# Fused attention and gated MLP: w_out reaches the DRAM scratch whole and early, and the maxima get other places in VectorE's order

## The chip, the cores and the metric

One core of a Trainium2 chip runs the kernel. The metric is the device time of one execution in microseconds. The kernel before was timed three times: median 730.39 us, from 729.67 to 731.17.

## What is computed

For 8 batches of 8 heads, 576 tokens and head width 64, a pack of 32 queries `p` attends to the tokens, and the tokens then attend to that pack. The result, laid out as 4608 x 512, goes through a gated MLP with d_ff = 2048.

```python
p_packed = sm_attn(p, k, v)
out = sm_attn(q, p_packed, p_packed)
x = out.transpose(0, 2, 1, 3).reshape(B * S, H * D)
h = x @ w_in
sp = np.maximum(h, 0.0) + np.log1p(np.exp(-np.abs(h)))     # softplus
return (h * erf(sp)) @ w_out
```

## The kernel before

**Units.** The second attention is folded into the first weight: W' = packed values times `w_in` (`wp`, L545), and h = a2 W' (L592). A unit is a batch b, a half c of its tokens and a block i of 256 columns of d_ff; `step(n, ...)` computes h of unit n, starts its gate and adds the products of earlier gates with `w_out` into the output accumulators (`o_part`, L644). An operand is split into a high and a low part, and a product is three matmuls.

**Two regimes.** Batches 0 and 1 (units 0 to 31) take softplus and erf from the tables in groups (L607, L610, gate L614) and fp32r splits of `w_out`: `wohl[f]` holds `wo_hi[f]` and `wo_lo[f]`, f = 0 to 15. Batches 2 to 7 take a gate of three tanh (L673 to L682) and 16-bit splits `woh[i]`, two blocks f to each. The 16-bit splits need scales: the largest absolute value of `w_in` (`tops_in`), of `w_out` (`tops_out`) and of the batch's packed values (`norm`). A maximum is gathered on DVE (`gather`), turned to a row by a PE transpose and cut to a power of two (`turn`), and spread over the partitions by a matmul (`spread`). `rho` scales W' of a batch, `sigma` the whole of `w_out`.

**How w_out comes and goes.** A block is loaded into a staging tile, its buffer `wo[f]` is cleared on POOL (L154), ACT casts the upper words (L123), DVE sets the rest (L127), and `split_w_out_high` and `split_w_out_low` make the parts. `wo`, `wohl`, the staging tiles, and later `wox` and `woh`, share the 18 buffers tagged "wo". In steps 20 to 23 `save` writes the block to a DRAM scratch: the high part by a DMA on SP, the low part by an accumulating DMA on POOL over the same rows. `whole` (L244) reads two blocks back as `wox[i]` in steps 24 to 27, and `halve` (L249 on ACT, L250 on DVE) makes `woh[i]`.

**Order.** `BEGINNING` is an order written out by hand for the work of units 0 to 19. After it, `plan` hangs parts on four slots of a step: slots 0 and 1 behind the first accumulation of the step, slot 3 behind the third, slot 2 at the step's end; `ATTEND` does it for the attention of a batch. PE, DVE and ACT keep the order in which the program issues their work; SP keeps it in BEGINNING only. POOL's order is a scheduler's. The outputs of batches 0 and 1 leave by DMAs on POOL (`outT<-ob`, L659 and L661), those of the second turn accumulating; `ob` has four buffers. The PSUM pool `ps_h` has two banks for h, for rows and columns of the maxima, and for some of the attention's scores; `ps_m` holds one tile.

Of the kernel before, what the change touches and what calls it, by code (L numbers as in the profile page):

```python
# [8 lines left out]
F32 = mybir.dt.float32  # L9
# [6 lines left out]
ALU = mybir.AluOpType  # L16
# [25 lines left out]
K12 S12 W1.3 W1.2 o11.0 o10.1 o11.1 o10.3 h15.0 H1.3 L14 F15 s14 V1.3 H1.2 T12 h15.1 L13 o11.3 p11.1 m12 U12 d15.1 M0 C  # L42
o10.2 o11.2 v12 c15.0 s15 h16.0 p11.2 p11.0 h16.1 c16.1 K14 m13 R14 o12.2 d16.0 s16 K13 S13 u13 v13 p11.3 e14 T13
o12.1 h17.0 h19.0 d19.0 o12.0 m14 e15 V1.2 m15 o12.3 e16 U14 v14 L15 K15 h17.1 c17.1 o13.1 o13.0 h19.1 c17.0 C c19.1
S15 o13.3 o14.1 h18.0 h18.1 m16 s19 s17 d18.0 C C C d18.1 M1 M2 M3 s18 e18 U15 o14.0 m18 e19 v15 e17 o13.2 o14.2 T15 m19 o14.3
m17 T14
"""

# [2 lines left out]
def tile_pack_attention_moe(ctx: ExitStack, tc: tile.TileContext, qT, kT, v, pT, w_in, w_out, outT):  # L51
    nc = tc.nc
    P = 128
    B, _, NC, S = qT.shape
    DFF = w_in.shape[1]
# [15 lines left out]
    NB0 = 2  # L71
# [9 lines left out]
    apool = ctx.enter_context(tc.tile_pool(name="attn", bufs=2))  # L81
# [10 lines left out]
    ones = cpool.tile([1, P], F32, name="ones")  # L92
    w_in_sb = cpool.tile([P, 4, DFF], F32, name="w_in_sb")
    scratch = dpool.tile([DFF, DM], F32, name="scratch")
    wo, wo_hi, wo_lo = {}, {}, {}
# [63 lines left out]
    def split_w_out_high(f, copy=nc.vector.tensor_copy):  # L159
        both = opool.tile([P, 2, DM], F32R, name=f"wohl{f}", tag="wo")  # L160
        wo_hi[f], wo_lo[f] = both[:, 0, :], both[:, 1, :]
        copy(wo_hi[f], wo[f])

    def split_w_out_low(f):
        nc.vector.tensor_tensor(wo_lo[f], wo[f], wo_hi[f], op=ALU.subtract)

    tops, inverse, halved, pairs = {}, {}, {}, {}
    rho, omega, gate_scales = {}, {}, {}

    def tallest(kind, k, src):  # L170

        if kind not in tops:
            tops[kind] = cpool.tile([P, 8 if kind == "in" else 16], F32, name=f"tops_{kind}")
        nc.vector.tensor_reduce(tops[kind][:, k:k + 1], src, axis=AX.X, op=ALU.max, apply_absolute_value=True)

    def tallest_in(k):

        tallest("in", k, w_in_sb[:, k // 2, (k % 2) * 2 * FB:(k % 2 + 1) * 2 * FB])

    def two_over(dst, src):  # L180

        nc.vector.tensor_reduce(dst, src, axis=AX.X, op=ALU.max)
        nc.vector.tensor_scalar(dst, dst, TINY, None, op0=ALU.max)
        bits = dst.bitcast(U32)
        nc.vector.tensor_scalar(bits, bits, EXPONENT, EXPONENT, op0=ALU.bitwise_and, op1=ALU.bitwise_xor)
# [22 lines left out]
    def other_way(dst, src):  # L208

        nc.vector.tensor_scalar(dst.bitcast(U32), src.bitcast(U32), EXPONENT, None, op0=ALU.bitwise_xor)  # L210

    def scales(b):

        rho[b] = apool.tile([P, 1], F32, name=f"rho{b}", tag="rho")
        nc.vector.tensor_scalar(rho[b][:], inverse[b][:], inverse["in"][:], 2.0 ** 11, op0=ALU.mult, op1=ALU.mult)
        back = apool.tile([P, 1], F32, name=f"back{b}", tag="back")
        other_way(back[:], rho[b][:])
        gate_scales[b] = apool.tile([P, 2], F32, name=f"gs{b}", tag="gs")
        nc.vector.tensor_scalar(gate_scales[b][:], consts[:], back[:], None, op0=ALU.mult)
        inverse[b] = back  # L220
# [8 lines left out]
    def out_weights():  # L229
# [1 line left out]
        nc.vector.tensor_scalar(sigma[:], inverse["out"][:], 2.0 ** 13, None, op0=ALU.mult)  # L231
        inverse["sigma"] = cpool.tile([P, 1], F32, name="inv_sigma")
        other_way(inverse["sigma"][:], sigma[:])

    def save(f):

        rows = scratch[f * P:(f + 1) * P, :]
        nc.sync.dma_start(rows, wo_hi[f].bitcast(F32))
        nc.gpsimd.dma_start(rows, wo_lo[f].bitcast(F32), accum_op=ALU.add)  # L239

    def whole(i):

# [14 lines left out]
    def in_turn(ins):  # L257

        if functions:
# [8 lines left out]

    ATTEND = {
# [52 lines left out]
    def attention(b):  # L322

        joined, third, roomy = b > NB0, b == NB0, b == 0
# [3 lines left out]
        def chunk(name, tag="kvq"):  # L328
            if tag == "kvq":
                return apool.tile([P, S], F32, name=f"{name}_{b}", tag="kvq", bufs=6)[:]  # L330
            if tag == "wo":
                return opool.tile([P, S], F32, name=f"{name}_{b}", tag="wo")[:]
            return tpool.tile([P, S], F32, name=f"{name}_{b}", tag=tag)[:]

        def bank(name, single=False):

            if single:
                return [ps_h.tile([P, 512], F32, name=f"{name}_{b}_{x}", tag="ps_h")[:] for x in range(2)], None
            if name in at_o:
                d = at_o[name]  # L340
                return [ps_o.tile([P, 512], F32, name=f"{name}_{b}_{x}", tag=f"ps_o{d + x}")[:] for x in range(2)], None
            ps = ps_m.tile([P, 2, 512], F32, name=f"{name}_{b}", tag="ps_m")
            return [ps[:, 0, :], ps[:, 1, :]], ps
# [10 lines left out]
        p = apool.tile([P, NC, NK], F32, name=f"p{b}", tag="p")  # L354
        nc.sync.dma_start(p[:], pT[b])
        k = [chunk(f"k{c}") for c in range(NC)]
# [76 lines left out]
        if roomy:  # L433
# [7 lines left out]
            po, pr = bank("p")[0]  # L441
# [56 lines left out]
        if b >= NB0:  # L498
            one = apool.tile([1, 1], F32, name=f"one{b}", tag="one")
            two_over(one[:], po[0:1, P:2 * P])  # L500
            yield
            nc.tensor.matmul(po[:, 2 * P:2 * P + 1], ones[:], one[:], start=True, stop=True)
            inverse[b] = apool.tile([P, 1], F32, name=f"inv{b}", tag="inv")
            nc.vector.tensor_copy(inverse[b][:], po[:, 2 * P:2 * P + 1])
        yield
        ta = apool.tile([P, 2, S], F32, name=f"ta{b}", tag="big", bufs=3)
        for c2 in range(2):
            banks = bank(f"s2_{c2}", b > NB0 + 1 or (b >= NB0 and c2 == 0) or (b == 1 and c2 == 1))
            for c in range(NC):
                for r in range(2):  # L510
                    nc.tensor.matmul(banks[0][r][NK * c:NK * c + NK, 0:HT], ptt[64 * r:64 * r + 64, NK * c:NK * c + NK],
                                     q[c][64 * r:64 * r + 64, c2 * HT:(c2 + 1) * HT], start=True, stop=True)
            yield
            if roomy:
                scores.append(banks[0])
            else:
                for r in range(2):
                    nc.vector.transpose(ta[:, r, c2 * HT:(c2 + 1) * HT], banks[0][r][:, 0:HT])
                yield
        tb = apool.tile([P, 2, S], F32, name=f"tb{b}", tag="big", bufs=3)  # L520
        kind = F32R if b < NB0 else F16
# [37 lines left out]
    def w_prime_high(b, j, copy=nc.scalar.copy):  # L559
        for hi, lo, ps in w_prime_parts(b, j):  # L560
            if b < NB0:
                copy(hi, ps)
            else:
                nc.scalar.mul(hi, ps, rho[b][:])
# [8 lines left out]
    raw, gs, rows, banks_of, ts = {}, {}, {}, {}, {}  # L573
# [205 lines left out]
    def slot(n, where):  # L779
        return plan.setdefault((n, where), [])  # L780

    for b in range(NB0, B):
        for j in range(NFB):
            n = JOINS[b][j] if b in JOINS else first_use[b] + (JOINS_LATER if b < B - 1 else PAIRED)[j]
# [6 lines left out]
            slot(n, where).append((attend, b))  # L791

    for k in range(4, 2 * NC):
        slot(19 + k // 2, 2).append((tallest_in, k))
    f = 0
    for n, count in ((22, 4), (23, 1), (24, 3), (25, 3), (27, 2), (28, 3)):
        for f in range(f, f + count):
            slot(n, 2).append((lambda f: tallest("out", f, wo_hi[f].bitcast(F32)), f))
        f += 1
    for n, where, part, kind in ((23, 2, gather, "in"), (24, 1, turn, "in"), (25, 0, spread, "in"),  # L800
                                 (28, 2, gather, "out"), (29, 1, turn, "out"), (30, 0, spread, "out")):
        slot(n, where).insert(0 if part == spread else len(slot(n, where)), (part, kind))
    slot(25, 2).insert(0, (scales, NB0))
    slot(30, 0).append((out_weights,))
    slot(32, 3).append((out_scale, NB0))
    for f in range(DFF // P):
        slot(20 + f // 4, 1).append((save, f))
    for i in range(NBLK):
        slot(24 + i // 2, 1).append((whole, i))
        slot(30 + i, 2).append((halve, i))  # L810
    for b in range(NB0 + 1, B):
        slot(first_use[b] - 6, 1).append((scales, b))
        slot(first_use[b] - 6, 1).append((out_scale, b))
# [29 lines left out]
    def fetch(*which):  # L843
# [4 lines left out]
        "N": lambda: next(halves["N"]), "X": lambda: next(halves["X"]),  # L848
        "F": fetch, "L": lambda *w: fetched[w][0](), "K": lambda *w: fetched[w][1](),
        "S": split_w_out_high, "T": split_w_out_low,  # L850
        "W": w_prime, "H": w_prime_high, "V": w_prime_low,
        "h": h_half, "c": h_copy, "s": softplus, "e": erf, "m": gate, "u": split_high, "v": split_low,
        "d": lambda n, k: h_copy(n, k, nc.vector.tensor_copy), "U": lambda n: split_high(n, nc.scalar.copy),
        "R": lambda f: split_w_out_high(f, nc.scalar.copy), "G": lambda b, j: w_prime_high(b, j, nc.vector.tensor_copy),
        "o": o_part, "p": put, "i": keep_busy, "M": tallest_in,
    }
    start = len(traced)
    for word in BEGINNING.split():
# [47 lines left out]
```

## Time and profile before

| What | us |
|---|---|
| median of 3 runs | 730.39 (729.67 to 731.17) |
| the profiled execution | 729.6 |
| its span | 727.8 |
| PE busy | 687.0 (94%) |
| DVE busy | 596.9 (82%) |
| ACT busy | 562.6 (77%) |
| POOL busy | 50.6 (7%) |
| mean granted PE clock | 0.981 |

The span is that of the instructions of the profiled execution; 1.8 us of its time lie around it. Busy shares are means over the whole span; the beginning, the stretch from 150 to 215 us and the regime of the tanh gates differ much from each other.

### The profile page before, as it was taken

To read this page: it belongs to the slowest core of one execution; us is meant where nothing else is said; L and a number is where in the kernel's file an instruction comes from. 1 tells how busy PE (TensorE), PEld (TensorE's weight loads), DVE (VectorE), ACT (ScalarE), POOL (GpSimd) and SP (SyncE) were. 2 spreads that over 40 slices of the span, in tenths; PEclk is the share of its full clock that TensorE was granted. 3 is DMA by queue.
4 is the path that set the end of the run, shared out by engine and by line. 5 is a ranking of instruction groups with operands and counts; after the bars stand their busy time and mean duration, and the time that the engine had idled before them with its cause. 6 is when DMAs were issued, how large, how long until landed. Compare 5 with 4: busy or idle time off the path is not lost.

```text
span 727.8 us, 15690 instructions
## 1 busy us (share of the span) xinstructions
PE 687.0 (94%) x6458; PEld 542.5 (75%) x6458; DVE 596.9 (82%) x945; ACT 562.6 (77%) x987; POOL 50.6 (7%) x75
## 2 busy tenths in 40 slices
PE   8899999988469989999999999999999999999997
PEld 6588989967459867786767777776767777677775
DVE  4999998687347799988997889888997889978775
ACT  2899888946167968988889778888889778878784
POOL 2011111123401100000000000000000000000000
PEclk9999999999779999999999999999999999999999
DMA  9955543299933230222011310222001200001000
GB/s 321 398 203 178 185 141 123 88 316 291 249 53 64 33 129 24 82 83 92 3 39 53 116 62 9 78 82 83 14 33 54 83 2 9 25 1 34 2 33 32
DMA packets 37639, 71.00 MB, mean 98 GB/s; under 512 B 4288, under 2 KB 13504, under 8 KB 37568
## 3 DMA queue, kind: packets, MB, share of 16 engines
q1 hardware_dynamic: 31904, 60.50, 24.6%
q0 software_dynamic: 5376, 8.92, 6.9%
q8 instruction: 50, 0.82, 0.5%
q10 hardware_dynamic: 288, 0.59, 0.2%
q14 instruction: 21, 0.17, 0.1%
HBM read 49.81 MB, written 20.19 MB: 96 GB/s over the span
## 4 chain that ended last, share of the span: by engine, by line
PE 39%; DVE 27%; ACT 21%; issue 6%; DMA 4%; POOL 2%; SPq 0%; POOLq 0%; ACTq 0%; DVEq 0%
PE o L644 22%; PE h L592 12%; DVE t L677 6%; DVE t L678 6%; ACT t L675 4%; ACT t L673 4%; DVE gl L627 3%; ACT u L676 3%; ACT t L680 3%; PE wp L545 3%; DVE hs L682 2%; POOL scratch L239 2%; DVE gh L620 2%; DMA wi<-w_in 2%; ACT ob L656 1%
## 5 line engine op out<-in xcount | busy, mean ns | idle before, releaser
L644 PE MATMUL o<-gh,woh 128*128 128x288 f16 x1536 | 304.9, 287 | 0.9 <-ACT ob L656 0.9
L644 PEld LDWEIGHTS <-woh 128*128 128x128 f16 x2304 | 223.8, 98 | 67.8 <-issue 11.7
L644 PE MATMUL o<-gl,woh 128*128 128x288 f16 x768 | 219.9, 286 | 0.5 <-DVE gl L627 0.4
L592 PE MATMUL h<-a2h,wph 128*128 128x288 f16 (+1 forms) x512 | 149.5, 292 | 3.9 <-ACT hs L600 2.7
L592 PE MATMUL h<-a2h,wpl 128*128 128x288 f16 (+1 forms) x512 | 148.5, 290 | 1.2 <-DVE wpl L569 1.2
L592 PE MATMUL h<-a2l,wph 128*128 128x288 f16 (+1 forms) x512 | 148.2, 289 | 0.0
L677 DVE SCALAR_TENSOR_TENSOR t<-hs,gs,t 128x576 f32<-128x576 f32 x96 | 78.1, 814 | 50.1 <-ACT u L676 49.5
L644 PE MATMUL o<-gh,wohl 128*128 128x288 f32 x448 | 100.2, 304 | 0.0
L602 ACT ACTIVATE hs<-h 128x288 f32<-128x288 f32 x192 | 71.7, 407 | 34.1 <-PE h L592 30.2
L627 DVE TENSOR_TENSOR gl<-hs,gh 128x576 f16<-128x576 f32 (+1 forms) x124 | 93.9, 758 | 4.8 <-ACT gh L620 0.8
L680 ACT ACTIVATE t<-t 128x576 f32<-128x576 f32 x96 | 65.8, 685 | 40.0 <-DVE t L678 38.6
L592 PEld LDWEIGHTS <-wph 128*128 128x128 f16 x768 | 74.7, 98 | 20.6 <-issue 1.6
L644 PEld LDWEIGHTS o<-gh,wohl 128*128 128x128 f32 x448 | 76.0, 192 | 5.8 <-issue 3.1
L678 DVE SCALAR_TENSOR_TENSOR t<-u,t 128x576 f32<-128x576 f32 x96 | 72.8, 758 | 3.3
L673 ACT ACTIVATE t<-hs,gs 128x576 f32<-128x576 f32 x96 | 73.8, 769 | 0.0
L682 DVE SCALAR_TENSOR_TENSOR hs<-t,hs 128x576 f32<-128x576 f32 x96 | 71.9, 749 | 1.0 <-ACT t L680 1.0
L620 DVE CAST gh<-hs 128x576 f16<-128x576 f32 (+1 forms) x117 | 53.3, 455 | 21.1 <-PE o L644 20.8
L675 ACT ACTIVATE t<-t 128x576 f32<-128x576 f32 x96 | 65.6, 683 | 3.0
L676 ACT ACTIVATE u<-t 128x576 f32<-128x576 f32 x96 | 65.6, 683 | 3.1
L644 PE MATMUL o<-gl,wohl 128*128 128x288 f32 x224 | 67.2, 300 | 0.0
L592 PEld LDWEIGHTS <-wpl 128*128 128x128 f16 x384 | 37.7, 98 | 9.7
L644 PEld LDWEIGHTS o<-gl,wohl 128*128 128x128 f32 x224 | 43.2, 193 | 0.3 <-DVE gl L627 0.2
(134 smaller groups left out, 834.7 us busy)
## 6 DMA issues: line engine op xcount, KB each, us to landing
q<-qT SPq DMA_DIRECT2D x32, 288.0 KB, 4.3
k<-kT SPq DMA_DIRECT2D x30, 288.0 KB, 5.0
wos<-w_out SPq DMA_DIRECT2D x16, 512.0 KB, 6.0
outT<-ob SPq DMA_DIRECT2D x48, 144.0 KB, 1.8
v<-v SPq DMA_DIRECT2D x24, 256.0 KB, 4.3
wi<-w_in SPq DMA_DIRECT2D x12, 512.0 KB, 6.4
outT<-ob POOLq DMA_DIRECT2D x32, 144.0 KB, 3.3
scratch<-wohl SPq DMA_DIRECT2D x16, 256.0 KB, 5.9
```

The costliest lines, as they stand in the source:

```text
L592: nc.tensor.matmul(ps[:, 0:HT], w[:, r, fo:fo + P], a[:, r, c * HT:(c + 1) * HT], start=(m == 0), stop=(m == 5))
L602: nc.scalar.mul(dst, src, 2.0 ** -19)
L620: copy(ghi[:], gs[n][0][:])
L627: nc.vector.tensor_tensor(glo[:], hs[:], ghi[:], op=ALU.subtract)
L644: nc.tensor.matmul(acc[b, c, d][:, 0:HT], w[f][:, d * P:(d + 1) * P], gg[:, k, :], start=(first and k == 0 and m == 0), stop=(last and k = ...
L673: nc.scalar.activation(t[:], hs[:], AF.Tanh, bias=T_BIAS, scale=scale[:, 0:1])
L675: nc.scalar.activation(t[:], t[:], AF.Square, bias=root * Q_BIAS, scale=root * Q_SCALE)
L676: nc.scalar.activation(u[:], t[:], AF.Tanh, bias=U_BIAS, scale=U_SCALE / A2)
L677: nc.vector.scalar_tensor_tensor(t[:], hs[:], scale[:, 1:2], t[:], op0=ALU.mult, op1=ALU.add)
L678: nc.vector.scalar_tensor_tensor(t[:], u[:], A1, t[:], op0=ALU.mult, op1=ALU.add)
L680: nc.scalar.activation(t[:], t[:], AF.Tanh, bias=A_BIAS, scale=A_SCALE)
L682: nc.vector.scalar_tensor_tensor(hs[:], t[:], 1.0, hs[:], op0=ALU.add, op1=ALU.mult)
```

## The change

Each block `wo[f]` goes to the scratch whole, by one plain DMA on POOL issued right behind the cast to its high part; the 16 writes on SP and the 16 accumulating DMAs on POOL of steps 20 to 23 are gone. The maxima get earlier places: two of `w_out` stand in BEGINNING, the others mostly a step or a slot earlier, `gather` of both kinds and `scales(2)` too, and `halve` moves to another slot of its step. In batch 2 the matmul that spreads the norm (`spread_norm`) is issued behind the first half of the second attention's scores, not ahead of it.

```diff
-S15 ... h18.1 m16 s19 s17 ...
+S15 ... h18.1 m16 O0 O1 s19 s17 ...
...
         copy(wo_hi[f], wo[f])
+        nc.gpsimd.dma_start(scratch[f * P:(f + 1) * P, :], wo[f])
...
+    def tallest_out(f):
+        tallest("out", f, wo_hi[f].bitcast(F32))
...
+    def spread_norm(b, po, one):
+        nc.tensor.matmul(po[:, 2 * P:2 * P + 1], ones[:], one[:], start=True, stop=True)
+        inverse[b] = apool.tile([P, 1], F32, name=f"inv{b}", tag="inv")
+        nc.vector.tensor_copy(inverse[b][:], po[:, 2 * P:2 * P + 1])
...
-    def save(f):
-        rows = scratch[f * P:(f + 1) * P, :]
-        nc.sync.dma_start(rows, wo_hi[f].bitcast(F32))
-        nc.gpsimd.dma_start(rows, wo_lo[f].bitcast(F32), accum_op=ALU.add)
...
             two_over(one[:], po[0:1, P:2 * P])
-            yield
-            nc.tensor.matmul(po[:, 2 * P:2 * P + 1], ones[:], one[:], start=True, stop=True)
...
+            if not third:
+                yield
+                spread_norm(b, po, one)
...
+            if third and c2 == 0:
+                spread_norm(b, po, one)
...
-        slot(19 + k // 2, 2).append((tallest_in, k))
+        slot(19 + k // 2, 1).append((tallest_in, k))
...
-    for n, where, part, kind in ((23, 2, gather, "in"), (24, 1, turn, "in"), (25, 0, spread, "in"),
-                                 (28, 2, gather, "out"), (29, 1, turn, "out"), (30, 0, spread, "out")):
+    for n, where, part, kind in ((22, 1, gather, "in"), (23, 1, turn, "in"), (24, 1, spread, "in"),
+                                 (28, 1, gather, "out"), (29, 1, turn, "out"), (30, 0, spread, "out")):
...
-    slot(25, 2).insert(0, (scales, NB0))
+    slot(24, 2).append((scales, NB0))
...
-        slot(20 + f // 4, 1).append((save, f))
...
-        slot(30 + i, 2).append((halve, i))
+        slot(30 + i, 3 if i == 0 else 1).append((halve, i))
```

**POOL, from the outputs of batch 0 in BEGINNING on.** Before, the last clearing of a `wo` buffer and eight outputs stand ahead of the saves of the low parts:

```order
L154 MEMSET wo_1385 128x512
L154 MEMSET wo_1405 128x512
L661 DMA outT<-ob_0_3_1_1414 128x288
L661 DMA outT<-ob_0_3_2_1458 128x288
L661 DMA outT<-ob_0_3_0_1461 128x288
L661 DMA outT<-ob_0_3_3_1493 128x288
L154 MEMSET wo_1545 128x512
L661 DMA outT<-ob_1_3_0_1723 128x288
```

With the change the saves stand between them:

```order
L154 MEMSET wo_1398 128x512
L154 MEMSET wo_1418 128x512
L667 DMA outT<-ob_0_3_1_1427 128x288
L667 DMA outT<-ob_0_3_2_1471 128x288
L163 DMA scratch<-wo_1398 128x512
L667 DMA outT<-ob_0_3_0_1474 128x288
L163 DMA scratch<-wo_1418 128x512
L667 DMA outT<-ob_0_3_3_1508 128x288
L154 MEMSET wo_1560 128x512
L163 DMA scratch<-wo_1560 128x512
L667 DMA outT<-ob_1_3_0_1742 128x288
```

All 16 saves now stand ahead of the second turn's outputs, which before had saves ahead of and between them; and some of the clearings have a save ahead of them.

**DVE in step 24, at the norm of batch 2** (`one` is the power of two of the norm, `inv` its copy spread over the partitions, `p` the PSUM tile that holds both). Before:

```order
L174 TENSOR_REDUCE tops_in<-w_in_sb 128x1 x2
L174 TENSOR_REDUCE tops_out<-wohl_682 128x1
L174 TENSOR_REDUCE tops_out<-wohl_720 128x1
L174 TENSOR_REDUCE tops_out<-wohl_802 128x1
L174 TENSOR_REDUCE tops_out<-wohl_765 128x1
L620 CAST gh_1_4_2017<-hs_1_4_1700 128x576
L627 TENSOR_TENSOR gl_1_4_2019<-hs_1_4_1700,gh_1_4_2017 128x576
L182 TENSOR_REDUCE one_2023<-p_1866 1x1
```

With the change:

```order
L175 TENSOR_REDUCE tops_out<-wohl_733 128x1
L187 TENSOR_REDUCE one_in<-row_in 1x1
L188 TENSOR_SCALAR one_in<-one_in 1x1
L190 TENSOR_SCALAR one_in<-one_in 1x1
L626 CAST gh_1_4_2012<-hs_1_4_1719 128x576
L633 TENSOR_TENSOR gl_1_4_2014<-hs_1_4_1719,gh_1_4_2012 128x576
L187 TENSOR_REDUCE one_2018<-p_1869 1x1
```

The reduction of the norm has one maximum and three single-row instructions where six maxima stood; those six are now further up.

**DVE in step 28, at the gathering of the maxima of w_out** (the three `hs<-t,hs` are the gates of the group that ends with this step). Before:

```order
L614 TENSOR_TENSOR hs_0_6_2233<-t_0_6_2260,hs_0_6_2233 128x576
L614 TENSOR_TENSOR hs_0_7_2288<-t_0_7_2337,hs_0_7_2288 128x576
L614 TENSOR_TENSOR hs_1_4_2368<-t_1_4_2394,hs_1_4_2368 128x576
L174 TENSOR_REDUCE tops_out<-wohl_1487 128x1
L174 TENSOR_REDUCE tops_out<-wohl_1474 128x1
L174 TENSOR_REDUCE tops_out<-wohl_1588 128x1
L190 TENSOR_REDUCE top_out<-tops_out 128x1
L182 TENSOR_REDUCE one_out<-row_out 1x1
```

With the change:

```order
L175 TENSOR_REDUCE tops_out<-wohl_1603 128x1
L195 TENSOR_REDUCE top_out<-tops_out 128x1
L626 CAST gh_0_5_2412<-hs_0_5_2130 128x576
L633 TENSOR_TENSOR gl_0_5_2414<-hs_0_5_2130,gh_0_5_2412 128x576
L620 TENSOR_TENSOR hs_0_6_2218<-t_0_6_2246,hs_0_6_2218 128x576
L620 TENSOR_TENSOR hs_0_7_2274<-t_0_7_2325,hs_0_7_2274 128x576
L620 TENSOR_TENSOR hs_1_4_2354<-t_1_4_2383,hs_1_4_2354 128x576
L187 TENSOR_REDUCE one_out<-row_out 1x1
```

`top_out`, which PE turns to `row_out`, stood behind the three gates and now stands ahead of them.

## Rows read from the trace of the kernel before

**Rows 1.** The page, busy time of each engine.
```profile
PE 687.0 (94%) x6458; PEld 542.5 (75%) x6458; DVE 596.9 (82%) x945; ACT 562.6 (77%) x987; POOL 50.6 (7%) x75
```

**Rows 2.** Waits of PE from 36 to 230 us: us in total, times, longest us.
```profile
PE row_out L196 <- DVE top_out L190: 17.3, 1, 17.3
PE p L502 <- DVE one L185: 3.0, 1, 3.0
PE h L592 <- ACT hs L600: 2.7, 1, 2.7
```

**Rows 3.** Timeline of DVE from 190 us (start, duration; in brackets the idle time before).
```profile
202.86 2.10 DVE L614 TENSOR_TENSOR hs<-t,hs 128x576 f32<-128x576 f32 x3 [14.07 <-ACT t L610]
...
206.77 0.17 DVE L190 TENSOR_REDUCE top_out<-tops_out 128x1 f32<-128x16 f32 x1
```

**Rows 4.** Timeline of ACT from 185 us.
```profile
196.65 0.40 ACT L654 COPY ob<-o 128x288 f32<-128x288 f32 x1 [10.59 <-DMA outT<-ob]
...
200.43 0.40 ACT L654 COPY ob<-o 128x288 f32<-128x288 f32 x1 [1.21 <-DMA outT<-ob]
...
203.88 0.68 ACT L600 COPY hs<-h 128x288 f32<-128x288 f32 x2
```

**Rows 5.** Timeline of POOL from 148 us.
```profile
150.34 2.70 POOL L239 DMA_DIRECT2D scratch<-wohl  x3 [15.37 <-DMA scratch<-wohl]
...
190.59 0.89 POOL L659 DMA_DIRECT2D outT<-ob  x1 [0.61 <-issue]
193.36 0.87 POOL L659 DMA_DIRECT2D outT<-ob  x1 [1.88 <-issue]
```

**Rows 6.** Stretches: length, busy time of PE, PEld, DVE, ACT, POOL, then granted clock, DMA share, GB/s.
```profile
150.00:172.00 22.00, 18.76 (x159) 15.86 (x158) 17.56 (x37) 9.09 (x16) 8.04 (x9) 0.92 1.08 292
172.00:180.00 8.00, 5.60 (x50) 3.93 (x50) 7.10 (x10) 5.19 (x8) 3.51 (x4) 0.79 1.10 303
207.00:214.00 7.00, 6.92 (x47) 6.50 (x55) 3.35 (x8) 1.40 (x3) 0.00 (x0) 0.80 0.00 0
```

**Rows 7.** DMA issues: number, KB each, median us from issue to landing.
```profile
outT<-ob POOLq DMA_DIRECT2D x32, 144.0 KB, 3.3
...
scratch<-wohl POOLq DMA_DIRECT2D x16, 256.0 KB, 7.3
wox<-scratch SPq DMA_DIRECT2D x8, 512.0 KB, 9.7
```

**Rows 8.** Timeline of DVE, from 98 to 122 us.
```profile
104.27 0.43 DVE L162 CAST wohl<-wo 128x512 fp32r<-128x512 f32 x1
...
112.82 0.43 DVE L162 CAST wohl<-wo 128x512 fp32r<-128x512 f32 x1
```

**Rows 9.** Timeline of ACT, from 98 to 122 us.
```profile
108.14 0.79 ACT L123 CAST wo<-wos 128x512 f16<-128x512 bf16 x1
...
116.86 0.78 ACT L123 CAST wo<-wos 128x512 f16<-128x512 bf16 x1
```

**Rows 10.** Timeline of POOL, from 60 to 150 us.
```profile
106.62 0.53 POOL L154 MEMSET wo<- 128x512 f32 x1 [2.40 <-DVE wohl L165]
```

**Rows 11.** Timeline of PE, three places.
```profile
155.06 0.46 PE L502 MATMUL p<-one,ones 1*128 1x1 f32 x2 [2.96 <-DVE one L185]
...
187.11 0.29 PE L644 MATMUL o<-gh,wohl 128*128 128x288 f32 x1
...
189.47 0.29 PE L644 MATMUL o<-gh,wohl 128*128 128x288 f32 x1
```

**Rows 12.** Timeline of DVE, from 153 to 158 us.
```profile
155.56 0.16 DVE L504 COPY inv<-p 128x1 f32<-128x1 f32 x1
```

**Rows 13.** Waits of PE from 230 to 300 us.
```profile
PE p L502 <- DVE one L185: 2.3, 1, 2.3
PE p L417 <- ACT a1t L469: 1.1, 1, 1.1
```

**Rows 14.** Groups of ACT by line, from 230 to 268 us (busy us, mean ns).
```profile
L249 ACT ACTIVATE woh<-wox,sigma 128x1024 f16<-128x1024 f32 x6 | 6.9, 1144 | 0.0
```

More of the change, by code (lines that the diff above doesn't have):

```diff
@@ L44 @@
 o12.1 h17.0 h19.0 d19.0 o12.0 m14 e15 V1.2 m15 o12.3 e16 U14 v14 L15 K15 h17.1 c17.1 o13.1 o13.0 h19.1 c17.0 C c19.1
-S15 o13.3 o14.1 h18.0 h18.1 m16 s19 s17 d18.0 C C C d18.1 M1 M2 M3 s18 e18 U15 o14.0 m18 e19 v15 e17 o13.2 o14.2 T15 m19 o14.3
+S15 o13.3 o14.1 h18.0 h18.1 m16 O0 O1 s19 s17 d18.0 C C C d18.1 M1 M2 M3 s18 e18 U15 o14.0 m18 e19 v15 e17 o13.2 o14.2 T15 m19 o14.3
 m17 T14
@@ L500, in attention @@
             two_over(one[:], po[0:1, P:2 * P])
-            yield
-            nc.tensor.matmul(po[:, 2 * P:2 * P + 1], ones[:], one[:], start=True, stop=True)
-            inverse[b] = apool.tile([P, 1], F32, name=f"inv{b}", tag="inv")
-            nc.vector.tensor_copy(inverse[b][:], po[:, 2 * P:2 * P + 1])
+            if not third:
+                yield
+                spread_norm(b, po, one)
         yield
@@ L793, in tile_pack_attention_moe @@
     for k in range(4, 2 * NC):
-        slot(19 + k // 2, 2).append((tallest_in, k))
-    f = 0
-    for n, count in ((22, 4), (23, 1), (24, 3), (25, 3), (27, 2), (28, 3)):
+        slot(19 + k // 2, 1).append((tallest_in, k))
+    f = 2
+    for n, count in ((22, 4), (23, 1), (24, 2), (25, 3), (26, 1), (27, 2), (28, 1)):
         for f in range(f, f + count):
-            slot(n, 2).append((lambda f: tallest("out", f, wo_hi[f].bitcast(F32)), f))
+            slot(n, 1).append((tallest_out, f))
         f += 1
-    for n, where, part, kind in ((23, 2, gather, "in"), (24, 1, turn, "in"), (25, 0, spread, "in"),
-                                 (28, 2, gather, "out"), (29, 1, turn, "out"), (30, 0, spread, "out")):
-        slot(n, where).insert(0 if part == spread else len(slot(n, where)), (part, kind))
-    slot(25, 2).insert(0, (scales, NB0))
+    for n, where, part, kind in ((22, 1, gather, "in"), (23, 1, turn, "in"), (24, 1, spread, "in"),
+                                 (28, 1, gather, "out"), (29, 1, turn, "out"), (30, 0, spread, "out")):
+        slot(n, where).append((part, kind))
+    slot(24, 2).append((scales, NB0))
     slot(30, 0).append((out_weights,))
     slot(32, 3).append((out_scale, NB0))
-    for f in range(DFF // P):
-        slot(20 + f // 4, 1).append((save, f))
     for i in range(NBLK):
         slot(24 + i // 2, 1).append((whole, i))
-        slot(30 + i, 2).append((halve, i))
+        slot(30 + i, 3 if i == 0 else 1).append((halve, i))
     for b in range(NB0 + 1, B):
@@ L854, in tile_pack_attention_moe @@
         "R": lambda f: split_w_out_high(f, nc.scalar.copy), "G": lambda b, j: w_prime_high(b, j, nc.vector.tensor_copy),
-        "o": o_part, "p": put, "i": keep_busy, "M": tallest_in,
+        "o": o_part, "p": put, "i": keep_busy, "M": tallest_in, "O": tallest_out,
     }
```

2 rows, old and new, of the table ATTEND are left out of this document.

## Prediction

> **What bounds the kernel now.** The page comes first: PE is busy 94% of the span [rows 1], so little outside PE's own work can matter except where PE stands still. The second view is therefore PE's waits by stretch. From 36 to 230 us there are three that count, 23.0 us in all: `row_out` for `top_out` 17.3, `p<-one` for `one` 3.0, and h for an ACT copy 2.7 [rows 2]. The third view follows the large one back. DVE reaches `top_out` only at 206.77, because the three gates ahead of it start at 202.86, after 14.07 us in which DVE stood idle for erf on ACT [rows 3]. ACT was late because its output copies waited for `ob` buffers: 10.59 us ahead of the one at 196.65, and again ahead of the one at 200.43 [rows 4]. Those buffers wait for output DMAs on POOL, and POOL could issue them only at 190.59 and later, at the end of a row of 16 saves that began at 150.34 [rows 5]. So the chain is: saves on POOL, output DMAs, `ob`, erf, gates, `top_out`, PE. The other two waits are an order on DVE: `one` stands behind maxima, and the h wait is an ACT copy behind `wph`, which waited for `rho`, another small DVE instruction behind gates and maxima.
>
> The last view is the granted clock. It falls to its lower level, 1.2 of 2.4 GHz, around each of these waits and returns some us later: the mean is 0.92 over 22 us, 0.79 over 8 and 0.80 over 7 [rows 6]. What is lost is (1 - 0.92) x 22 = 1.8, 0.21 x 8 = 1.7 and 0.20 x 7 = 1.4, together 4.8 us in which PE worked slowly after having stood still.
>
> **The large wait.** The 16 accumulating saves on POOL and the 16 writes on SP go. In their place 16 plain DMAs on POOL stand in BEGINNING, which ends well ahead of the 150.34, and where POOL has little else. The second turn's outputs then find an empty queue; an output lands in 3.3 us [rows 7], and the four buffers serve the four outputs of one half of the tokens at a time, with a whole half's products between them; so neither `ob` nor erf waits. Besides, `top_out` no longer stands behind the gates. Either of the two would take most of the 17.3 us; both are made. I count 17.3 out, and its 1.4 us of clock.
>
> What is late next there: `row_out` needs a bank of `ps_h`, and the one it gets is freed by the ACT copy of h of the step. ACT does the last output copy, the table load and three erfs ahead of that copy: 203.88 - 200.43 = 3.45 us, and the copy takes 0.40 (an output copy of the same 128x288 [rows 4]). The product ahead of the output copy starts on PE at 187.11 and takes 0.29; with 0.14 us from engine to engine (`top_out` ends 206.94, and PE's wait of 17.3 ends at 207.08) ACT starts at 187.54, and `row_out` may start at 187.54 + 3.45 + 0.40 + 0.14 = 191.5. PE comes there when its work behind 189.47 + 0.29 ends, at 189.8 [rows 11]. So a wait of 1.7 us stays.
>
> **The two small waits.** `one` has one maximum ahead of it instead of six, and `spread_norm` is issued behind the scores' first half, which covers it: 3.0 out, 1.8 of clock with it. `spread_norm` now writes the `ps_m` tile into which the scores' second half goes, so PE waits for the copy `inv`: matmul at 155.06, copy from 155.56 to 155.72 [rows 11, 12], 0.7 us new. `rho` stands ahead of the gates, so `wph` and the ACT copy don't wait: 2.7 out, 1.7 of clock. `col_out` moves behind `s_1_3` and takes a bank that an ACT copy frees: 0.40 + 0.14, about 0.6 us new. The maxima themselves cost the same wherever they stand; in the new places DVE had idle time, and where it hadn't, PE asks for nothing that stands behind them.
>
> **The saves in their new place.** SP loses 16 issues, which nothing waited for but the reads of `wox`; these now go out earlier, and `woh` is wanted only by unit 32. On POOL a save keeps `wo[f]` until it has landed, and that buffer is cleared again for a later block. This makes two clearings late. DVE casts a block at 104.27 and another at 112.82, 0.43 each [rows 8]; the next clearings that take those buffers take 0.53 us each on POOL, the first today at 106.62 [rows 10], and ACT's casts behind them at 108.14 and 116.86 [rows 9]. With a landing of L us, the casts can start at 104.70 + L + 0.53 and 113.25 + L + 0.53, which is L - 2.9 and L - 3.1 late. The trace has no plain POOL write of 256 KB. From below it is 3.3 us (144 KB out, plain or accumulating), from above 7.3 (256 KB accumulating) [rows 7]; I take 5.0, nearer the lower one, since the traffic of 292 GB/s in which the 7.3 was measured [rows 6] isn't there. That makes 2.1 + 1.9 = 4.0 us of delay on ACT, with bounds of 0.6 and 8.6. Queued behind the casts on ACT are copies of h and casts of gates, for which PE waits in the end; PE has no wait above 0.2 us in that stretch and other products to do, so I charge 1.5 us, with bounds 0 and 8.6.
>
> A rule of the Trainium skill speaks against this place: the page "SBUF — State Buffer", section "SBUF: two separate sides", says that a DMA issued by GpSimd has its descriptors written through a port that VectorE holds during its two-port operations, so that it is late by as much, and gives 3.1 us against 0.62; as an estimate from that page a save would land 2.5 us later, and the sum would be 5 us higher. The rows speak for another cause of POOL's slow issue: between the outputs at 190.59 and 193.36 lie 1.88 us of "issue" while DVE was idle (its 14.07 us before 202.86) [rows 3, 5]. The sum goes without the rule.
>
> **halve.** Its ACT half moves ahead of the first tanh of the step: 1.14 us each [rows 14]. What is put ahead of the tanh delays the gate, and what stood behind it delayed the copy of h. PE waits 2.3 + 1.1 = 3.4 us in that region, for `one` and for `a1t` [rows 13]. I leave this as it is. From below all of it goes (3.4 gained); from above six such instructions of 1.14 lie on the gate's path, 6.9 us lost.
>
> **Sum.** Out: 23.0 of waits + 4.8 of clock = 27.8 us. New: 1.7 + 0.7 + 0.6 + 1.5 = 4.5. Gain 23.3 us. The profiled execution of before took 729.6, so one of after takes 706.3; the median of three runs was 0.8 above that execution, so I forecast 707.1, say 707 us.
>
> **Rivals.**
> 1. *Everything goes.* The new waits are covered, and the earlier `wox` and `halve` take the waits of the region of `halve` too: 27.8 + 3.4 = 31.2 us, and 729.6 - 31.2 + 0.8 gives 699 us. For it: `woh` is ready earlier. Against it: `row_out` waits for a bank whose release I can count out, and the waits there are for attention, not for `woh`. Chance 0.12.
> 2. *halve takes it back.* ACT has no idle time ahead of these instructions from 230 to 268 us [rows 14]; six times 1.14 in the gate's path give 707 + 6.9 = 714 us, with PE's clock down once more 716. Against it: the copy of h gains what the tanh loses. Chance 0.18.
> 3. *The bubble stays in part*, since outputs on POOL are paced at some 2 to 2.8 us each even without saves between them (190.59 to 193.36). If the group's erf is late by half of the 17.3, the time is about 716 us. Against it: `top_out` is ahead of the gates, so only the gates' products would wait. Chance 0.05.
> 4. *Slower.* A save lands so late that the two clearings stop ACT, and with it PE, in 104 to 120. It costs 2L - 6.0. To undo 27.8 - 3.0 (the other new waits) = 24.8 us, L must be over 15.4 us; with L = 18 it is 735 us. The slowest DMAs of the trace, the reads of `wox`, land in 9.7 at twice the size [rows 7]. Chance 0.04. At L of 14 to 15 the change would not show: 0.02.
>
> My forecast holds 0.59: its own range is 702 to 712. What tells from no change is about 0.2%, 1.5 us. The range with 8 in 10 reaches into rivals 1 and 2: 698 to 715. Faster 0.94, same 0.02, slower 0.04.
>
> **What would show it.** After: no wait of PE above 2 us from 36 to 230 us; POOL without a DMA of `scratch` behind BEGINNING's end; ACT's output copies without a wait for `outT`; `row_out` waiting 1 to 2 us for a bank, not for `top_out`; clock 1.0 at 150 to 215. Right for the wrong reason would be a bubble that is gone while the waits at 100 to 120 have grown. Wrong would be: POOL's clearings waiting for `scratch` by 5 us and more with PE standing still behind them, or waits of PE for `gl` in 230 to 270, the sign that `halve` lengthens the gate.

## The result, and the profile after

The changed kernel takes 706.06 us (median of 4 runs, 705.58 to 706.21); beside it on the same chip the kernel before took 730.78 (729.67 to 733.11). The ratio is 0.9657, with a 95% interval from 0.9632 to 0.9681: 24.7 us faster. The forecast was 707 us, with a gain of 23.3.

The page after, busy time of each engine and the granted clock by slices (span 704.4 us):

```profile
PE 682.3 (97%) x6458; PEld 539.4 (77%) x6458; DVE 596.9 (85%) x945; ACT 563.1 (80%) x987; POOL 44.8 (6%) x75
...
PEclk9999999999999999999999999999999999999999
```

DVE has just the busy time that it had, ACT half a microsecond more; nothing was done with less work there. PE is busy 4.7 us less than in [rows 1], near the 4.8 that the forecast took as lost at the lower clock. Where it is less is shown further down: 4.1 between the two norms, 1.5 behind them, and 0.9 more ahead of them.

PE's waits from 36 to 225 us, to be read against [rows 2]:

```profile
PE row_out L201 <- ACT hs L606: 1.5, 1, 1.5
PE h L598 <- DVE wpl L575: 0.7, 1, 0.7
PE h L598 <- ACT hs L606: 0.7, 1, 0.7
PE col_out L209 <- ACT a L357: 0.6, 1, 0.6
PE o L650 <- DVE gl L633: 0.4, 1, 0.4
PE s L515 <- DVE inv L221: 0.2, 1, 0.2
```

The wait of 17.3 us for `top_out` is gone, and `row_out` now waits 1.5 us for an ACT copy of h, the one that frees its bank. (The 0.7 us for `wpl` lies at the seam of the stretch, near 36 us, and belongs to the start-up.) The stretches, to be read against [rows 6]:

```profile
150.00:172.00 22.00, 21.67 (x201) 19.05 (x209) 19.17 (x38) 14.55 (x24) 3.54 (x4) 1.00 0.86 284
172.00:180.00 8.00, 8.00 (x85) 7.26 (x69) 7.42 (x12) 4.77 (x10) 1.16 (x2) 1.00 0.01 3
```

The clock is 1.00 in both, and from 150 to 215 us as a whole. ACT at the place of [rows 4]:

```profile
178.90 0.39 ACT L660 COPY ob<-o 128x288 f32<-128x288 f32 x1
179.60 0.40 ACT L660 COPY ob<-o 128x288 f32<-128x288 f32 x1 [0.30 <-PE o L650]
180.39 0.40 ACT L660 COPY ob<-o 128x288 f32<-128x288 f32 x1 [0.39 <-PE o L650]
180.81 1.28 ACT L616 ACT_TABLE_LOAD   x1
182.10 1.83 ACT L616 ACTIVATE t<-t 128x576 f32<-128x576 f32 x3
183.84 0.68 ACT L606 COPY hs<-h 128x288 f32<-128x288 f32 x2
```

The output copies wait for PE, not for `outT`. From the last of them to the copy of h it is the same 3.45 us as before, which the forecast used: the first half ends at 184.24, and `row_out` starts at 184.27.

Whole runs start unevenly: PE comes to the turning of batch 2's norm at 150.1 us in this trace and at 149.6 to 152.0 in others with the same beginning. A stretch between two events on PE is steadier than the whole. An earlier transpose, the norm of batch 2 and the norm of batch 3, before (first fence) and after (second):

```profile
49.11 0.27 PE L491 MATMUL p<-ident,a 128*128 128x128 f32 x1
...
148.65 0.27 PE L493 MATMUL p<-ident,norm 128*1 128x128 f32 x1 [0.18 <-DVE norm L489]
...
258.96 0.27 PE L493 MATMUL p<-ident,norm 128*1 128x128 f32 x1
```

```profile
49.44 0.27 PE L496 MATMUL p<-ident,a 128*128 128x128 f32 x1
...
150.08 0.27 PE L498 MATMUL p<-ident,norm 128*1 128x128 f32 x1 [0.18 <-DVE norm L494]
...
237.10 0.27 PE L498 MATMUL p<-ident,norm 128*1 128x128 f32 x1
```

From norm to norm it was 110.3 us and is 87.0: 23.3 us of the gain lie here. The changed kernel is 1.4 us later where the stretch begins. Of this, 0.3 are there at the earlier transpose and belong to the uneven start; the other 1.1 are a cost of the early saves, for from that transpose to the norm it is 99.5 us in all four traces without them, and 100.6 in seven of the ten with them, 101.3, 101.7 and 102.6 in the other three. The end of the span is 23.4 us earlier, so 1.5 us more are gained behind batch 3's norm.

### The profile page after: what moved, and what is told of

Same layout as the page of the kernel before. It is cut to its first block, busy times and chain, and to the rows that moved or that the text cites. A ratio compares the mean times of both kernels' runs of the same rounds, so it can differ in the third digit from the quotient of the medians.

```text
span 704.4 us, 15671 instructions
## 1 busy us (share of the span) xinstructions
PE 682.3 (97%) x6458; PEld 539.4 (77%) x6458; DVE 596.9 (85%) x945; ACT 563.1 (80%) x987; POOL 44.8 (6%) x75
## 4 chain that ended last, share of the span: by engine, by line
PE 44%; DVE 26%; ACT 22%; issue 4%; DMA 2%; POOL 1%; ACTq 0%; DVEq 0%; POOLq 0%
PE o L650 25%; PE h L598 13%; DVE t L683 6%; DVE t L684 6%; ACT t L681 4%; ACT t L679 4%; DVE gl L633 4%; ACT u L682 3%; ACT t L686 3%; PE wp L551 3%; DVE gh L626 2%; DVE hs L688 2%; ACT ob L662 1%; ACT hs L608 1%; PE s L515 1%
## 5 line engine op out<-in xcount | busy, mean ns | idle before, releaser
L650 PE MATMUL o<-gh,wohl 128*128 128x288 f32 x448 | 98.3, 300 | 0.0
L650 PEld LDWEIGHTS o<-gh,wohl 128*128 128x128 f32 x448 | 74.3, 188 | 5.5 <-issue 1.8
```

What stands on the lines that cost most here:

```text
L650: nc.tensor.matmul(acc[b, c, d][:, 0:HT], w[f][:, d * P:(d + 1) * P], gg[:, k, :], start=(first and k == 0 and m == 0), stop=(last and k = ...
```

## The experiments

**The early saves alone.** The kernel before, with its orders of DVE and ACT untouched.

```diff
         copy(wo_hi[f], wo[f])
+        nc.gpsimd.dma_start(scratch[f * P:(f + 1) * P, :], wo[f])
...
-        slot(20 + f // 4, 1).append((save, f))
```

> The kernel before with the 16 early plain saves on POOL alone; the maxima, rho, spread_norm and halve stand where they stood. If the row of saves on POOL is the head of the chain (output DMAs, ob, erf), the 17.3 us wait of row_out shrinks to about 4.2 us: the bank's wait of 1.5 us, and 2.5 us more since top_out stands behind the last gate and three maxima. The waits for one (3.0) and for h (2.7) stay, with 3.5 us of clock. That gives 706.1 + 5.7 - 0.3 + 3.5 + 2.5 + 1.4 (clock of the wait of 4.2) = about 719 us. The rival, that the order of the maxima makes the bubble, expects 725 us or more here.

Measured: 718.96 us (715.49 to 720.60), ratio 0.9823 (0.9787 to 0.9859). PE's waits:

```profile
PE p L497 <- DVE one L186: 5.2, 2, 2.9
PE row_out L197 <- DVE top_out L191: 4.3, 1, 4.3
PE h L587 <- ACT hs L595: 3.3, 2, 2.7
```

The wait of `row_out` shrinks to 4.3 us with the order of DVE as it was: the old saves were the head of that chain. The other two of [rows 2] stay as they were (2.9 of the 5.2, and 2.7 of the 3.3).

**No accumulating saves.** The kernel before without the 16 low parts; the high parts still go out on SP in steps 20 to 23. The 16-bit splits of w_out lack the low parts here.

```diff
         nc.sync.dma_start(rows, wo_hi[f].bitcast(F32))
-        nc.gpsimd.dma_start(rows, wo_lo[f].bitcast(F32), accum_op=ALU.add)
```

> The kernel before without its 16 accumulating DMAs on POOL, so that the scratch holds only the high parts and the 16-bit splits of w_out lack the low parts. If POOL's in-order queue is what delays the output DMAs, this is like the early saves alone: row_out waits some 4 us, about 719 us. If the traffic of the saves or the 16 writes on SP are the cause, the outputs stay late and the time is above 727 us.

Measured: 715.85 us (714.87 to 717.49), ratio 0.9798 (0.9777 to 0.9818). `row_out` waits as long as with the early saves:

```profile
PE p L501 <- DVE one L185: 5.3, 2, 3.0
PE row_out L196 <- DVE top_out L190: 4.3, 1, 4.3
PE h L591 <- ACT hs L599: 2.7, 1, 2.7
```

So it is the 16 DMAs in POOL's queue, not SP's writes and not traffic as such: from 150 to 182 us 311 GB/s are moved here (second fence), at a DMA share of 0.93, and ACT's output copies have no wait for `outT`. That this kernel is faster than the one above is for the most part a matter of the clock. Both have the same large waits of PE; from 150 to 182 us the clock is 0.81 in the one profiled execution (first fence, the early saves alone) and 0.95 in the other, 0.14 x 32 = 4.5 us. The four runs of each bear it out: the early saves alone took 720.4 and 720.6 us at mean clocks of 0.986 and 0.988, and 715.5 and 717.5 at 0.993, while this kernel took 714.9 to 717.5 at 0.990 to 0.995.

```profile
150.00:182.00 32.00, 26.20 (x188) 22.94 (x187) 26.18 (x49) 14.70 (x25) 3.51 (x4) 0.81 0.63 201
```

```profile
150.00:182.00 32.00, 26.20 (x234) 22.85 (x233) 25.37 (x47) 16.56 (x28) 3.52 (x4) 0.95 0.93 311
```

**The order alone.** The changed kernel with the old saves.

```diff
-        nc.gpsimd.dma_start(scratch[f * P:(f + 1) * P, :], wo[f])
...
+        slot(20 + f // 4, 1).append((save, f))
```

> The changed kernel with the old saves: high parts on SP, accumulating low parts on POOL, in steps 20 to 23. The prediction's sentence that either of the two would take most of the 17.3 us expects 707 to 712 us. Against it: row_out still needs the bank that the ACT copy of h frees, and that copy stands behind the output copies that wait for POOL; then row_out goes only from 207.1 to about 204.4, whatever was saved ahead of it, because POOL's row of saves ends at the same time, and the time is 727 to 728 us.

Measured: 721.01 us (720.60 to 722.66), ratio 0.9870 (0.9851 to 0.9889): neither the 707 to 712 us of the one side nor the 727 to 728 of the other. PE's waits, and POOL around the outputs:

```profile
PE row_out L200 <- ACT hs L611: 5.6, 1, 5.6
PE s L398 <- DMA k<-kT: 4.5, 2, 3.6
```

```profile
181.19 0.86 POOL L670 DMA_DIRECT2D outT<-ob  x1 [1.17 <-issue]
184.21 0.88 POOL L670 DMA_DIRECT2D outT<-ob  x1 [2.15 <-ACT wph L575]
186.26 0.87 POOL L249 DMA_DIRECT2D scratch<-wohl  x1 [1.17 <-issue]
188.92 0.86 POOL L670 DMA_DIRECT2D outT<-ob  x1 [1.79 <-ACT ob L665]
191.20 0.89 POOL L249 DMA_DIRECT2D scratch<-wohl  x1 [1.42 <-issue]
```

POOL's order is the scheduler's, and with the new program it put three more outputs between the saves, at 181 to 189 us. They had stood behind the last save, from 190.59 on [rows 5]. So this run changed two things. The loads of k are a new wait: SP issues them from 164.71 us on, behind the 16 writes that it begins at 146.34, and PE comes to them sooner.

**The order alone, with POOL's order of before.** The same kernel; a dependency without a semaphore sets the outputs behind the last save.

```diff
-            nc.gpsimd.dma_start(where, ob[:], accum_op=ALU.add)
+            out = nc.gpsimd.dma_start(where, ob[:], accum_op=ALU.add)
+            if b + c + d:
+                then(out.ins, saved[-1])
```

> The changed kernel with the old saves and POOL's order as in the kernel before (the second turn's outputs, all but the first, behind the last save; in order_only the scheduler had put three of them between the saves). If the output copies that wait for POOL, and the bank freed behind them, set row_out whatever top_out does, row_out resumes at 203 to 206 us and the time is 726 to 729 us. If the early top_out is worth something by itself, it stays at the 721 us of order_only.

Measured: 728.08 us (727.70 to 729.64), ratio 0.9985 (0.9976 to 0.9995). PE's wait, and ACT ahead of it:

```profile
PE row_out L200 <- ACT hs L613: 15.3, 1, 15.3
```

```profile
197.22 0.40 ACT L667 COPY ob<-o 128x288 f32<-128x288 f32 x1 [12.02 <-DMA outT<-ob]
...
200.36 0.40 ACT L667 COPY ob<-o 128x288 f32<-128x288 f32 x1 [1.98 <-DMA outT<-ob]
...
203.81 0.68 ACT L613 COPY hs<-h 128x288 f32<-128x288 f32 x2
```

The last output copy starts at 200.36 and the copy of h at 203.81, against 200.43 and 203.88 [rows 4]. `top_out` is no longer what is waited for, and 15.3 us remain, for the bank. The row of saves on POOL ends when it did, so whatever time is saved ahead of `row_out` is spent waiting there: the order is worth 1.6 us by itself (728.08 against 729.71).

**top_out behind the gates, with the early saves.**

```diff
-(28, 1, gather, "out")
+(28, 2, gather, "out")
```

> The changed kernel with top_out gathered behind the gates, as before. By the prediction (either of the two takes most of the 17.3) and by the early saves alone, where row_out waited 4.3 us: 4.3 instead of 1.5 us here, 2.8 us more, and 1.4 to 1.8 us more if PE's clock falls after it: 709 to 711 us. If the saves alone were all of it: 706 us.

Measured: 708.20 us (707.93 to 710.90), ratio 0.9719 (0.9696 to 0.9742). `row_out`:

```profile
PE row_out L201 <- DVE top_out L195: 2.4, 1, 2.4
```

The wait is 2.4, not the 4.3 that was expected: the three maxima that stood between the gates and `top_out` are elsewhere in the new order, and at 0.6 us each they are the 1.9 of difference. From norm to norm the edit costs 2.4 us (89.4 against 87.0): 0.9 of waiting, and the clock after it, 0.95 from 182 to 215 us in the profiled execution (0.05 x 33 = 1.7).

**The saves on SP's queue.**

```diff
-        nc.gpsimd.dma_start(scratch[f * P:(f + 1) * P, :], wo[f])
+        nc.sync.dma_start(scratch[f * P:(f + 1) * P, :], wo[f])
```

> The changed kernel with the 16 early saves issued by SP instead of POOL. The page's rule (descriptors of a DMA issued by POOL are held up by DVE) expects earlier landings, no late clearing of buffers and 0.7 us less, 705 us. The rival: SP's queue is in order, each save waits there for its block's cast, and the loads of w_in, w_out, k and v behind it go out later: 707 to 712 us, with PE or ACT waiting for DMAs between 40 and 125 us.

Measured: 706.86 us (705.79 to 707.43), ratio 0.9691 (0.9673 to 0.9708): no difference from the changed kernel that these runs can tell, and 87.0 us from norm to norm. A save lands in 2.7 us (median) from SP (first fence) as from POOL in the changed kernel (second):

```profile
scratch<-wo SPq DMA_DIRECT2D x16, 256.0 KB, 2.7
```

```profile
scratch<-wo POOLq DMA_DIRECT2D x16, 256.0 KB, 2.7
```

Neither side comes out. The clearings are late from SP too: one waits 7.9 us for a save to land, and ACT's cast behind it 3.1 us, where it waits 3.0 in the changed kernel. SP did wait for the blocks (24.8 us in eight waits on DVE's part of `wo`), but PE has no wait for a DMA from 36 to 140 us, so the loads behind them had that much to spare.

**Two edits that go on from the change.** `row_out` and `col_out` each two accumulations later in their step, so that PE has work while ACT frees the banks; and `halve` where it was.

```diff
-(29, 1, turn, "out"), (30, 0, spread, "out")
+(29, 3, turn, "out"), (30, 3, spread, "out")
...
-    slot(30, 0).append((out_weights,))
+    slot(30, 3).append((out_weights,))
...
-        slot(30 + i, 3 if i == 0 else 1).append((halve, i))
+        slot(30 + i, 2).append((halve, i))
```

The second edit alone, and then both:

> The changed kernel with halve at the end of its step, as before. The prediction counted the move at nothing: 706 us, within 1 us. Rival 1 of the prediction (the move takes waits away) expects up to 3.4 us more than the changed kernel, rival 2 (the move lengthens the gate's path) up to 6.9 us less.

> The changed kernel with row_out and col_out each two accumulations later in their step, and halve at the end of its step. If the two waits are only for the banks that ACT frees meanwhile, 1.5 and 0.6 us of PE's waits go, and 1.3 us of the waits from 215 to 250 us with halve: 706.1 - 3.4 = 702.7 us. If the banks then hold up h instead, or the later sigma holds up halve, 705 to 707 us.

Measured: 705.80 us (704.20 to 706.55) for `halve` alone, 702.18 us (701.58 to 703.73) for both. Then the four kernels on one chip:

> The changed kernel once more, for a comparison of four kernels on one chip: 706 us.

> The changed kernel with halve at the end of its step, beside the changed kernel on one chip. By PE's waits in the two traces (4.6 against 3.4 us from 215 to 250 us) it is 1.3 us faster, 704.7 us; by the first two medians, taken on different chips, 0.3 us.

> The changed kernel with row_out and col_out each two accumulations later, halve as the change has it. The waits of 1.5 and 0.6 us go: 2.1 us faster than the changed kernel, 703.9 us. If sigma's later arrival holds up the first woh, less.

> Both edits, beside the others on one chip: 1.3 + 2.1 = 3.4 us faster than the changed kernel, 702.6 us; if the two overlap, some 704 us.

| On one chip | median us | range | ratio to before | norm to norm in its trace, us |
|---|---|---|---|---|
| the changed kernel | 706.64 | 705.70 to 707.85 | 0.9680 (0.9660 to 0.9701) | 87.0 |
| halve at the step's end | 706.05 | 705.46 to 706.60 | 0.9671 (0.9652 to 0.9691) | 85.5 |
| row_out and col_out later | 704.04 | 703.88 to 705.20 | 0.9647 (0.9628 to 0.9667) | 85.5 |
| both | 703.65 | 703.50 to 705.28 | 0.9638 (0.9620 to 0.9657) | 83.4 |

The later rows and columns give 2.6 us by the medians, and the waits of 1.5 and 0.6 us are gone from the trace; from norm to norm they give 1.5, and 2.1 with `halve` at the step's end. For `halve` the medians show 0.4 to 0.6 us, which is less than their ranges. The two norms on PE with `halve` at the step's end:

```profile
149.88 0.27 PE L498 MATMUL p<-ident,norm 128*1 128x128 f32 x1 [0.18 <-DVE norm L494]
...
235.36 0.27 PE L498 MATMUL p<-ident,norm 128*1 128x128 f32 x1
```

They are 85.5 us apart, and again in the second trace on another chip (152.00 to 237.50); the changed kernel has 87.0 in both of its traces (the second: 150.60 to 237.64). So `halve` in its new place costs 1.5 us there, and 2.1 with the later rows and columns. Much of it comes back in the clock: with `halve` at the step's end PE waits 2.3 us for batch 3's `one`, and on the one chip eight of the nine runs of these two kernels have a mean clock of 0.998, while those with the change's place have 0.999 and 1.000. A difference of 0.002 is 1.4 us in 704, so it can account for the little that the medians show.

## Why the prediction held, step by step

**The chain.** Its head and its end were shown by runs: without the accumulating DMAs on POOL `row_out` waits 4.3 us instead of 17.3; with them, and with the outputs behind them, it waits 15.3 us even when `top_out` is early. The links between them, the output copies, erf and the gates, are read from the traces. The signs that the forecast named are there: no wait of PE above 2 us from 36 to 225, POOL's last save at 121 us, output copies that don't wait for `outT`, 1.5 us for a bank at `row_out`, and a clock of 1.00 from 150 to 215 us.

**"Either of the two would take most of the 17.3 us"** is wrong for one of the two. The early saves do it alone. The early `top_out` does not: the bank's release stands behind the same output copies, and 15.3 us remain. The forecast named that bank just behind, as what is late next, and did not see that it is late by nearly as much as long as the saves are there. For the same reason the two small waits were not to be had alone: they lie ahead of `row_out`, and with the old saves what they give is waited away there. So the parts do not add up one by one. The order alone is worth 1.6 us, the early saves alone 11.3 (718.96 against 730.29 beside it), and the order on top of the early saves 13.2 more (705.80 on the same chip, with `halve` left where it was). As both edits were made, the sum did not suffer.

**The new waits.** `row_out` 1.5 (1.7 forecast), `col_out` 0.6 (0.6), the copy `inv` 0.2 (0.7). The last was mis-sized: in the trace behind [rows 11, 12] DVE had a maximum and `top_in` ahead of `inv`, and in the new order nothing, so the copy follows its matmul at once. The late clearings of `wo` cost 1.1 us (1.5 forecast) from the transpose at 49 us to batch 2's norm. As a wait of PE, 0.7 of it shows, h for an ACT copy at 110.8, which stands in the traces with early saves and in none without them; in two of these traces a second one, at 121 us, adds 0.8 and 1.6. The size was taken from a landing of 5.0 us, within 3.3 to 7.3; the landing is 2.7 (median), below both bounds. The lower bound was a median over two kinds, which the trace of before has apart (plain outputs from 50 to 140 us, accumulating ones from 150 to 260):

```profile
outT<-ob POOLq DMA_DIRECT2D x16, 144.0 KB, 2.4
```

```profile
outT<-ob POOLq DMA_DIRECT2D x16, 144.0 KB, 4.1
```

The plain ones alone would have given 2.4, and the 2.7 would have lain within the bounds. (The Trainium skill, page "DMA: Bandwidth & Descriptors", section "Anatomy of one DMA — SWDGE (gpsimd) path", gives 2.0 us and the bytes at 436 GB/s; as an estimate from that page 262144 bytes take 2.6 us, and the trace agrees with 2.7.)

The form was partly another, too: by the forecast's own formula, L - 2.9, a landing of 2.7 us makes nothing late. ACT's longest wait for a clearing after the change, 1.58 us before it, is

```profile
105.96 0.79 ACT L123 CAST wo<-wos 128x512 f16<-128x512 bf16 x1 [2.99 <-POOL wo L154]
```

and the clearing ahead of it didn't wait for a landing; it stood in POOL's queue behind a save that itself waited for its block on DVE:

```profile
104.85 0.54 POOL L163 DMA_DIRECT2D scratch<-wo  x1 [1.25 <-DVE wo L127]
105.38 0.55 POOL L154 MEMSET wo<- 128x512 f32 x1
107.27 0.53 POOL L154 MEMSET wo<- 128x512 f32 x1 [1.34 <-DMA scratch<-wo]
```

The next one, and one at 118.08, waited for a save to land. Together the new costs are 1.5 + 0.6 + 0.2 + 1.1 = 3.4 us where 4.5 were forecast.

**The rule on POOL's descriptors** (the Trainium skill, page "SBUF — State Buffer", section "SBUF: two separate sides") would have made the early saves land later than from SP. No run here shows it: 2.7 us (median) from either queue, in a stretch in which DVE is busy nine tenths of the time. How much of that is in the two-port operations of which the rule speaks was not counted.

**halve** was counted at nothing, with bounds from 3.4 gained to 6.9 lost. It costs 1.5 us from norm to norm, rival 2's direction at a quarter of its price, and the wait for `gl` that the forecast named as its sign is there. PE's waits there grew from the 3.4 us of [rows 13] to 4.6: 2.3 for `one` became 1.1 for `one` and 1.1 for `inv`, the 1.1 for `a1t` stayed, and 0.4 for `gl` and 0.9 for an output copy came to them. The clock, 0.91 from 250 to 270 us in the kernel before (0.09 x 20 = 1.8 us), is 1.0 after, and 1.5 us are gained behind batch 3's norm; the forecast had left this out of its sum. That it is the change's is not shown. The old place of `halve` has the same wait of 2.3 us in seven traces: in two (before, and one with both edits) the clock falls behind it and 468.8 us follow batch 3's norm; in five it doesn't, and 467.0 to 467.2 follow, about what follows after the change (467.3).

**In sum**, 23.3 us were forecast, counted from the profiled execution of before; 23.4 lie between it and that of after (729.6 and 706.2), and the medians add what runs of one kernel differ by. The waits that went are 23.0 us as counted, and the clock between the norms gave 4.1 back, not 4.8. New costs are 3.4, not 4.5, and the uneven start takes 0.3. That makes 23.0 + 4.1 - 3.4 - 0.3 = 23.4 by itself. So the path of the forecast held and its sizes were near. The last tenths are luck, though: `halve` takes 1.5 and the clock behind batch 3's norm gives 1.5, and neither stood in the sum.

## What to carry to other kernels

When one wait ends late, list all that the waiting instruction needs, the bank as well as the data, and follow each back: two of them here led to the same queue, so the new order bought 1.6 us while that queue was full and some 13 once it was empty. Waits that lie ahead of such a place cannot be added up as if each stood alone. Look for work that shares an in-order queue with something urgent, and move it to where the queue is empty; whether the early saves went out on POOL or SP made no difference here. To weigh an edit of 1 or 2 us, compare two events inside one trace that enclose it, since the starts of whole runs differ by more, and then look at the clock behind the second event, which can take the gain back.

## What the runs showed of the hardware that was not expected

The same wait does not always bring the clock down for the same time. Two traces with the same three waits of PE, 2.9 to 3.0, 2.7 and 4.3 us, have 0.81 and 0.95 as the granted clock from 150 to 182 us, and with the early saves alone the time varies from 715.49 to 720.60. A wait of 2.3 us for batch 3's `one` cost no clock in a trace of `halve` at its old place (1.00 from 215 to 250 us, first fence), but did in one of the kernel with both edits (0.95, second fence), which is some of what that kernel varies by, 702.18 us at a mean clock of 1.000 on one chip and 703.65 at 0.998 on another:

```profile
215.00:250.00 35.00, 31.63 (x345) 25.26 (x344) 31.83 (x53) 29.20 (x51) 3.54 (x4) 1.00 0.37 92
```

```profile
215.00:250.00 35.00, 31.63 (x332) 24.57 (x332) 31.28 (x52) 27.56 (x49) 3.53 (x4) 0.95 0.37 92
```

A plain save of 256 KB landed in 2.7 us and took POOL 0.54 us to issue (medians); the accumulating one took 7.3 [rows 7] and 0.87, and both carry the same bytes. POOL's time goes with the kind: an accumulating output of 144 KB takes it 0.86 to 0.89 us in the changed kernel too, from 200 to 230 us, where only 37 GB/s are moved, and a plain output of that size 0.54. In the landing the crowd has a large share: in the kernel before, SP's plain writes of 256 KB, issued from 144 to 158 us, landed in 5.9 us. That is another queue, so how much of the rest is the kind's stays open.

```profile
scratch<-wohl SPq DMA_DIRECT2D x16, 256.0 KB, 5.9
```
